# A planner's order with later loads, a table of 24 shifted tasks, and the last tile stored in two halves

## The chip, the cores and the metric

The kernel runs on one core of a Trainium2 chip. The metric is the time of one execution on the device in microseconds, the median of five runs. A profile is one further execution, taken by the hardware profiler; PE is the matrix engine (TensorE), DVE is VectorE, ACT is ScalarE, POOL is GpSimd, SP is SyncE, which issues most DMAs.

## What is computed

```python
for t in range(S):                                   # r, k, v: (4, 8, 768, 48); w, u: (8, 48)
    kt, vt, rt = k[:, :, t], v[:, :, t], r[:, :, t]
    cur = einsum('bhd,bhe->bhde', u * kt, vt)
    y[:, :, t] = einsum('bhd,bhde->bhe', rt, state + cur)
    state = w * state + einsum('bhd,bhe->bhde', kt, vt)
x = y.transpose(0, 2, 1, 3).reshape(4, 768, 384)
xn = (x - mean(x)) / sqrt(var(x) + 1e-6) * g_ln
out = x + maximum(xn @ w_ch1, 0) @ w_ch2             # w_ch1: 384 x 1536, w_ch2: 1536 x 384
```

A linear attention with a decaying state, then a layer norm and a two-layer network with a residual.

## The kernel before

The 4 x 768 rows are cut into 24 tiles of 128 tokens (i = 0 to 23, six to a batch). Within a tile the recurrence is written as matrix products: k and r are scaled by powers of the decay (tables Fk and Fr, made at the start from a scan, transposed on PE and copied to SBUF by ACT, L301 to L310), transposed, multiplied to a 128 x 128 score per head, masked, and multiplied with v; a 48 x 48 state per head goes from tile to tile.

For each tile the tasks are, in the names that the planner gives them: **k, r, v** loads (r for two tiles at once); **sck, scr** scale k and r (L365, L368); **TK, TR** transpose them on PE (L380, L394); **kT, rT** copy the transposed tiles out of PSUM (L386, L401); **vc** casts v to bf16 (L373); **q** multiplies r and k for the bonus term, **cc** sums it on PE, **cp** copies it out (L451), **Vb** multiplies v with it on POOL; **at** are the scores on PE (L417), **A** masks them on DVE; **kv** and **S, Z** update the state; **y** is the sum on PE (L508), **x** adds the bonus (L535). Then **xn** centres x, **sq** and **rs** give the variance, **ln** and **lc** transpose xn: for tiles under 8 on PE with a copy by ACT (L612), for the later ones as a DMA transpose that SP issues (L606). **up** g_m is one unit of the first product of group g (one tile for the first six groups, then two), six or twelve matmuls into a PSUM bank hp (L618); **re** is the relu that empties it, on ACT or DVE (L635); **dn** i m is a third of the second product of tile i, four matmuls of 384 columns (L649); **ot** scales and adds x on DVE (L662); **st** stores the tile (L673). The weights come in six loads, w1l and w2l, through four buffers, and are scaled or cast to bf16 in pieces (w1s, w2s). dn needs the matching third of w2.

PSUM has little room: one bank each for transposes (tr), scores (at), bonus and state (s), y and the second product (o), two for hp.

The order is not written by hand. Each task has an engine, a cost, needs, the buffers it takes and gives, a priority and sometimes other engines it may run on (alt). Planner.order (L47) is a list scheduler: again and again it takes the task that can start first by its costs, with the priority to break ties, puts it behind what its engine already has, and emits the instructions in that order. It runs when the kernel is built. On the chip every engine, SP's DMA queue too, works off its own list strictly in order, waiting on semaphores; so a task that waits for a load holds back everything after it on its engine. A load's end is planned as the time when the DMA engines have moved it plus `lands` (1.9 us, L109). SLK and SLT add a slack, which is 0 before. `after` holds a task back in the plan; it is no wait on the chip.

Where the plan leaves PE a gap before the first dn, matmuls on an identity are put in (keep_warm, L266 and L816 to L819).

Of the kernel before, what the change touches and what calls it, by code (L numbers as in the profile page):

```python
# [9 lines left out]
FP32 = mybir.dt.float32  # L10
# [4 lines left out]


RA = [("DVE", 0.64)]
SLK, SLT = 0.0, 35.0
PACE = 4.4


class Planner:
# [12 lines left out]
    def add(self, name, eng, cost, fn, needs=(), takes=(), gives=(), pri=0, load=0.0, kind=None,  # L35
            alt=None, lands=1.9, after=0.0):

        t = dict(name=name, eng=eng, cost=cost, fn=fn, needs=list(needs), takes=list(takes),  # L40
                 gives=list(gives), pri=pri, load=load, kind=kind, alt=alt, lands=lands, end=None,
                 first=(eng, cost), after=after)
        self.tasks.append(t)
        assert name not in self.by_name, name
        self.by_name[name] = t

    def order(self, patience=0.0, spread=0.0, seed=0):  # L47
# [14 lines left out]
        out = []  # L62
        while todo:
            best = None
            for t in todo:
                data = t["after"]
                ok = True
                for n in t["needs"]:
                    d = self.by_name[n]
                    if d["end"] is None:  # L70
                        ok = False
                        break
                    lag = 0.0 if d["eng"] == t["eng"] else self.LAG[d["eng"]]
                    if t["eng"] == "PE" and d["eng"] not in ("PE", "") and eng_at["PE"] > SLT:
                        lag += SLK
                    data = max(data, d["end"] + lag)
                if not ok:
                    continue
                for b, _, _ in t["takes"]:
                    if not free_at[b]:  # L80
                        ok = False
                        break
                    data = max(data, min(free_at[b]))
                if not ok:
                    continue
                pri = t["pri"] + vary[family[t["name"]]]
                if t["kind"] is not None and t["kind"] == last_kind:
                    pri -= 0.5
                pick = None
                for eng, cost in [(t["eng"], t["cost"])] + (t["alt"] or []):  # L90
                    ready = max(data, eng_at[eng] if eng else 0.0)
                    if t["load"]:
                        ready = max(ready, dma_at - (3.0 if eng == "SP" else 2.0))
                    if pick is None or ready + cost < pick[0]:
                        pick = (ready + cost, ready, eng, cost)
                key = (pick[1] - (patience * pri if pick[2] in ("DVE", "ACT", "POOL") else 0.0), -pri)
                if best is None or key < best[0]:
                    best = (key, t, pick)
            assert best is not None, [t["name"] for t in todo][:20]
            t, (_, t0, eng, cost) = best[1:]  # L100
            t["eng"], t["cost"] = eng, cost
            todo.remove(t)
            if t["kind"] is not None:
                last_kind = t["kind"]
            end = t0 + t["cost"]
            if t["eng"]:
                eng_at[t["eng"]] = end
            if t["load"]:
                dma_at = max(dma_at, end + 1.2) + t["load"]  # L109
                end = dma_at + t["lands"]  # L110
            t["start"], t["end"] = t0, end
            for b, owner, uses in t["takes"]:
                slots = free_at[b]
                slots.remove(min(slots))
                held[b, owner] = [uses, 0.0]
            for b, owner in t["gives"]:
                h = held[b, owner]
                h[0] -= 1
                h[1] = max(h[1], end)
                if h[0] == 0:  # L120
                    free_at[b].append(h[1] + self.LAG[t["eng"]])
            out.append(t)
# [4 lines left out]
def kernel(  # L127
# [173 lines left out]
    Fr = const.tile([P, 2, H, D], FP32, name="Fr")  # L301
    Fk = const.tile([P, H, D], FP32, name="Fk")
    LH = L // 2
    for j in range(3):
        fps = ps_h.tile([P, 512], FP32, name="hp") if j < 2 else ps.tile([P, 512], FP32, name="y")
        for kc in range(CK):
            src = T2[:, kc] if j == 2 else T[:, kc, j : 2 * L : 2]
            nc.tensor.transpose(out=fps[:, kc * P : (kc + 1) * P], in_=src, identity=ident_f[:])
        src = fps[:, :C].rearrange("p (h d) -> p h d", h=H)
        nc.scalar.copy(out=Fr[:, j] if j < 2 else Fk[:], in_=src)  # L310
    vec = const.tile([P, NR], FP32, name="vec")
    vps = ps.tile([P, 512], FP32, name="s")
    w_p, u_p = vec[:, CK : CK + HP], vec[:, CK + HP : NR]
# [80 lines left out]
    def transposes_r(e):  # L394
        sc = r_bufs[e % NSR].rearrange("p j (q e) d -> p j q (e d)", e=2)
        tp_t[e] = ps.tile([P, 2 * HP, P], BF16, name="tr")
        for j in range(2):
            for q in range(HP):
                nc.tensor.transpose(out=tp_t[e][:, j * HP + q, :], in_=sc[:, j, q, :], identity=ident[:])  # L399

    def evacuate_r(i, eng):  # L401
        e, c = divmod(i, 2)
        rT_t[i] = trp.tile([P, HP, P], BF16, name="rT", bufs=NRT)
        (eng.copy if eng is nc.scalar else eng.tensor_copy)(  # L404
            out=rT_t[i][:].rearrange("p q (t j) -> p q j t", j=2),
            in_=tp_t[e][:, :, c * LH : (c + 1) * LH].rearrange("p (j q) t -> p q j t", j=2),
        )
# [40 lines left out]
                skip_group_check=True,  # L448
            )

    def bonus_copy(i):  # L451
        cc_t[i] = sb2.tile([P, H], FP32, name="cc")
        nc.scalar.copy(out=cc_t[i][:], in_=s_t[i][:, C : C + H])  # L453

    def bonus_value(i):
        Vb_t[i] = sb2.tile([P, H, D], FP32, name="Vb")
# [152 lines left out]
            xT_t[g] = sb3.tile([P, CK, GW], BF16, name="xT")  # L609
        nc.sync.dma_start_transpose(out=xT_t[g][:, :, j * P : (j + 1) * P], in_=xn_t[i][:])  # L610

    def ln_evacuate(i):  # L612
        g, j = tile_group[i]
        nc.scalar.copy(out=xT_t[g][:, :, j * P : (j + 1) * P], in_=tp_t[i][:, :CK, :])

    hp_t = {}

    def up(g, m):  # L618
        gw = group_len[g] * P
        nf = 512 // gw  # L620
        if m == 0:
            hT_t[g] = sb3.tile([P, FK, GW], BF16, name="hT", bufs=NH)
        hp_t[g, m] = hp = ps_h.tile([P, 512], FP32, name="hp")
        for f in range(nf):
# [48 lines left out]
    def store(i, eng):  # L673
        b, c = divmod(i, NCH)
        eng.dma_start(out=out[b, c * L : (c + 1) * L, :], in_=ot_t[i][:])


    plan = Planner(
        dict(wst=NWS, sck=NSC, scr=NSR, r=LR, k=LD, vf=LD, vv=LD, tr=1, at=1, s=1, y=1, hp=2, o=1, kT=NKT, rT=NRT, q=2, A=2, cc=2, Vb=2,
             Z=3, S=2, x=NX, sum=4, sqs=4, sq=2, xn=3, xT=3, hT=NH, ot=3)  # L680
    )
    add = plan.add
    NU = {g: FK * n * P // 512 for g, n in enumerate(group_len)}
    add("scan", "DVE", 5.65, None, pri=99)
    add("Fr", "ACT", 5.9, None, pri=99)
    add("Fk", "ACT", 0.65, None, needs=["Fr"], pri=99)
    for name, lands in (("r0", 5.4), ("k0", 6.4), ("v0", 7.5), ("rows", 5.5)):
        add(name, "", lands, None, pri=99, takes={"r0": [("r", 0, 2)], "k0": [("k", 0, 1)], "v0": [("vf", 0, 2)]}.get(name, []))
    add("turn", "PE", 0.15, turn_rows, needs=["rows", "Fk", "TR0", "TK0"], pri=70, takes=[("s", "vec", 1)])
# [33 lines left out]
    for i in range(NT):  # L723
# [8 lines left out]
        if not half:  # L732
            add(f"scrb{e}", "", 0.0, None, [], [("scr", e, 1)], pri=p0)
            for t in range(2):
                add(f"scr{e}{t}", "POOL", 1.1, lambda g, e=e, t=t: scale_r(e, t, g), [f"r{e}", "Fr", f"scrb{e}"], [],
                    [("r", e)], pri=p0, alt=[("DVE", 0.7)])
            add(f"TR{e}", "PE", 0.46, lambda e=e: transposes_r(e), [f"scr{e}0", f"scr{e}1"], [("tr", ("r", e), 2)],
                [("scr", e)], pri=p0)
        add(f"rT{i}", "ACT", 0.74, lambda g, i=i: evacuate_r(i, g), [f"TR{e}"] + (["kT0"] if i == 1 else []), [("rT", i, 1)], [("tr", ("r", e))], pri=p0,
            alt=[("DVE", 0.74)])  # L740
# [3 lines left out]
                alt=[("DVE", 0.44)])  # L744
        else:
            add(f"kT{i}", "SP", 1.25, lambda i=i: transpose_k_by_dma(i), [f"sck{i}"], [("kT", i, 2)], [("sck", i)], pri=80,
                load=0.67, lands=3.0)
        add(f"vc{i}", "POOL", 0.6, lambda e, i=i: cast_v(i, e), [f"v{i}"] + ([f"kT{i}", f"rT{i}"] if i < 2 else []), [("vv", i, 1 if last else 2)],
            [("vf", i)], pri=p0, alt=[("ACT", 0.53), ("DVE", 0.42)])
        if qp(i):  # L750
# [2 lines left out]
        else:  # L753
# [2 lines left out]
        add(f"at{i}", "PE", 0.47, lambda i=i: scores(i), [f"kT{i}", f"rT{i}"], [("at", i, 1)], [("kT", i)], pri=p0 + 1)  # L756
        add(f"cc{i}", "PE", 0.13, lambda i=i: bonus(i), [f"q{i}", "uw"], [("s", i, 1 if last else 2)],
            [("q", i)], pri=p0 + 1)
        add(f"cp{i}", "ACT", 0.2, lambda i=i: bonus_copy(i), [f"cc{i}"], [("cc", i, 1)], [("s", i)], pri=p0 + 1)
        add(f"Vb{i}", "POOL", 0.85, lambda i=i: bonus_value(i), [f"cp{i}", f"v{i}"], [("Vb", i, 1)],  # L760
            [("cc", i), ("vf", i)], pri=p0 + 1)
        add(f"A{i}", "DVE", 1.22, lambda i=i: masked(i), [f"at{i}"], [("A", i, 1)], [("at", i)], pri=p0 + 1)
# [29 lines left out]
        if i < LNP:  # L792
            add(f"ln{i}", "PE", 0.18, lambda i=i: ln_transposes(i), [f"xn{i}", f"xT{g}"], [("tr", ("l", i), 1)],
                [("xn", i)], pri=p0 + 2)
            add(f"lc{i}", "ACT", 0.5, lambda i=i: ln_evacuate(i), [f"ln{i}"], [], [("tr", ("l", i))], pri=p0 + 2)
        else:
            add(f"lc{i}", "SP", 1.2, lambda i=i: ln_by_dma(i), [f"xn{i}", f"xT{g}"], [], [("xn", i)], pri=90, load=0.5, lands=3.0)
        for m in range(NM):
            add(f"dn{i}{m}", "PE", 0.66, lambda i=i, m=m: down(i, m),
                [f"re{g}_{u}" for u in range(NU[g])] + [f"w2s{m}{f}" for f in range(FS)] + ([f"dn{i}{m - 1}"] if m else []),  # L800
# [3 lines left out]
        add(f"st{i}", "SP", 0.55, lambda e, i=i: store(i, e), [f"ot{i}"], [], [("ot", i)], pri=99, load=0.6, lands=1.8,  # L804
            alt=[("ACT", 0.5)])
    for g, n in enumerate(group_len):
        for m in range(NU[g]):
            f0, f1 = m * FK // NU[g], (m + 1) * FK // NU[g] - 1
            w = sorted({f0 // FB, f1 // FB})
            add(f"up{g}_{m}", "PE", 0.66, lambda g=g, m=m: up(g, m),  # L810
                [f"lc{group_first[g] + j}" for j in range(n)] + [f"w1s{q}{kc}" for q in w for kc in range(CK)],
                [("hp", (g, m), 1)] + ([("hT", g, n)] if m == 0 else []), [("xT", g)], pri=-40, kind="u")
            add(f"re{g}_{m}", "ACT", 0.6, lambda e, g=g, m=m: relu(g, m, e), [f"up{g}_{m}"], [], [("hp", (g, m))], pri=30, alt=RA)
    pe_at = 6.1
    for t in plan.order():
        if t["eng"] == "PE":  # L816
            gap = t["start"] - pe_at - 0.1
# [36 lines left out]
```

## Time and profile before

| what | us |
|---|---|
| median of 5 runs (lowest to highest) | 158.59 (158.09 to 158.9) |
| the profiled execution | 159.96 |
| its span, first to last instruction | 158.2 |
| PE busy | 147.5 (93%), 1851 matmuls |
| of it warming matmuls | 12.8, 152 matmuls |
| DVE, ACT, POOL busy | 116.5, 97.3, 85.5 |
| granted clock of PE | 0.999 |

```profile
PE   5999999889999998989899959999999999999990
...
DMA  4999989999989989999798899212021211111122
```

The span is cut into 40 slices of about 4 us, and a digit is the busy share in tenths. PE is nearly full from the second slice on, with slices of 8 in between; the DMA engines are nearly full until slice 25, when the loads are done. Matmuls are pipelined and their ends are modelled, so the start to start distance of PE's rows is a better price than their duration. A row of the timeline is: start, duration, engine, line, operation, tiles, count, and in brackets the idle time before it and what ended it.

### The profile page before, as it was taken

Reading aid. Unit: us, or ns where it says so; the run is one execution under the profiler, and the core shown is the slowest. Engines: PE = TensorE matmul, PEld = TensorE weight load, DVE = VectorE, ACT = ScalarE, POOL = GpSimd, SP = SyncE. Lnnn points to the kernel's source line nnn. Section 1 sums busy time; section 2 is a strip of 40 time slices with the busy share of each in tenths; the row PEclk is TensorE's granted clock in tenths of the full one; section 3 lists DMA queues with packets and bytes.
Section 4 is the critical chain, followed back from the end, with each engine's and each line's share of the span. In section 5 each row is a group of like instructions: output and inputs, shape, how many; then the busy total and the mean of one; then the engine's idle time right before and its main releaser. Section 6 shows DMA issues by size and latency. Waiting matters only on the chain.

```text
span 158.2 us, 4634 instructions
## 1 busy us (share of the span) xinstructions
PE 147.5 (93%) x1851; PEld 115.8 (73%) x1851; DVE 116.5 (74%) x232; ACT 97.3 (62%) x217; POOL 85.5 (54%) x116
## 2 busy tenths in 40 slices
PE   5999999889999998989899959999999999999990
PEld 5899898668887776866677748787877777777650
DVE  5769999679798999888998949898999841001231
ACT  3558879757877686548877637677485454553100
POOL 7369598398647894695966668961642220000000
PEclk9999999999999999999999999999999999999999
DMA  4999989999989989999798899212021211111122
GB/s 98 233 227 341 348 164 265 377 188 182 250 195 240 229 192 176 235 234 212 154 240 173 186 204 206 77 29 75 4 85 64 57 47 49 50 54 50 50 99 99
DMA packets 75418, 25.46 MB, mean 161 GB/s; under 512 B 69632, under 2 KB 74246, under 8 KB 75398
## 3 DMA queue, kind: packets, MB, share of 16 engines
q1 hardware_dynamic: 72070, 23.21, 63.0%
q10 hardware_dynamic: 3232, 1.97, 4.1%
q8 instruction: 14, 0.23, 0.7%
q14 instruction: 6, 0.05, 0.1%
q0 software_dynamic: 96, 0.01, 0.1%
HBM read 18.88 MB, written 4.72 MB: 149 GB/s over the span
## 4 chain that ended last, share of the span: by engine, by line
PE 47%; DMA 27%; POOL 9%; SPq 8%; issue 3%; DVE 3%; ACT 1%; POOLq 0%; ACTq 0%
PE hp L627 18%; PE o L654 18%; DMA wst<-in_moe_w_ch_dram 11%; DMA v<-in_v_dram 11%; SPq L195 5%; DMA xT<-xn 3%; PE hp L654 2%; PE at L422 2%; DMA k<-in_k_dram 2%; POOL sc L369 2%; POOL Vb L457 2%; SPq L189 2%; PE y L525 1%; PE tr L399 1%; PE tr L384 1%
## 5 line engine op out<-in xcount | busy, mean ns | idle before, releaser
L627 PE MATMUL hp<-xT,w_sb 128*128 128x256 bf16 (+1 forms) x540 | 57.9, 251 | 0.7 <-DMA xT<-xn 0.6
L654 PE MATMUL o<-w_sb,hT 128*128 128x384 bf16 x264 | 52.1, 326 | 0.6 <-POOL w_sb L360 0.6
L627 PEld LDWEIGHTS <-w_sb 128*128 128x128 bf16 x540 | 43.4, 98 | 8.6 <-DMA xT<-xn 1.1
L641 ACT ACTIVATE hT<-hp 128x512 bf16<-128x512 f32 x60 | 35.5, 598 | 18.1 <-PE hp L627 17.5
L654 PEld LDWEIGHTS <-hT 128*128 128x128 bf16 x288 | 26.2, 98 | 13.6 <-issue 0.6
L664 DVE SCALAR_TENSOR_TENSOR ot<-o,rs,x 128x384 f32<-128x384 f32 x22 | 13.5, 612 | 22.4 <-PE o L654 22.3
L432 DVE TENSOR_TENSOR A<-at,mask 128x1024 bf16<-128x1024 f32 x24 | 29.2, 1215 | 0.5 <-PE at L422 0.4
L457 POOL TENSOR_TENSOR Vb<-v,cc 128x384 f32<-128x384 f32 x24 | 20.6, 856 | 9.1 <-ACT cc L453 9.1
L369 POOL TENSOR_TENSOR sc<-r,Fr 128x384 bf16<-128x384 f32 x18 | 19.8, 1112 | 7.9 <-ACT Fr L310 2.9
L366 POOL TENSOR_TENSOR sc<-k,Fk 128x384 bf16<-128x384 f32 x19 | 19.9, 1047 | 0.0
L565 ACT ACTIVATE sq<-x,sum 128x384 bf16<-128x384 f32 x24 | 14.6, 609 | 1.7 <-DVE x L538 1.6
L388 ACT COPY kT<-tr 128x512 bf16<-128x512 bf16 x22 | 12.9, 586 | 4.2 <-PE tr L384 3.1
L404 ACT COPY rT<-tr 128x512 bf16<-128x512 bf16 x17 | 11.8, 737 | 4.5 <-PE tr L399 2.8
L538 DVE SCALAR_TENSOR_TENSOR x<-y,Vb 128x384 f32<-128x384 f32 x24 | 13.1, 547 | 1.8 <-POOL Vb L457 1.4
L268 PE MATMUL o<-ident 128*128 128x128 bf16 x152 | 12.8, 240 | 1.6 <-DVE ident L243 1.6
L268 PEld LDWEIGHTS <-ident 128*128 128x128 bf16 x152 | 10.6, 109 | 1.9 <-DVE ident L243 1.6
L422 PE MATMUL at<-rT,kT 48*128 48x128 bf16 x192 | 9.5, 219 | 2.3 <-ACT kT L388 2.2
L422 PEld LDWEIGHTS <-kT 48*128 48x128 bf16 x192 | 5.4, 94 | 5.9 <-ACT kT L388 3.8
L643 DVE TENSOR_SCALAR hT<-hp 128x512 bf16<-128x512 f32 x12 | 8.2, 687 | 1.8 <-PE hp L627 1.7
L375 ACT CAST vv<-v 128x384 bf16<-128x384 f32 x10 | 5.1, 512 | 7.1 <-DMA v<-in_v_dram 7.0
L384 PE MATMUL tr<-ident,sc 128*128 128x128 bf16 x92 | 8.9, 219 | 0.5 <-DVE rT L404 0.5
L525 PE MATMUL y<-vv,A 128*128 128x48 bf16 x192 | 8.7, 183 | 0.4 <-DVE A L432 0.4
(87 smaller groups left out, 196.7 us busy)
## 6 DMA issues: line engine op xcount, KB each, us to landing
r<-in_r_dram SPq DMA_DIRECT2D x12, 384.0 KB, 5.0
k<-in_k_dram SPq DMA_DIRECT2D x24, 192.0 KB, 4.4
wst<-in_moe_w_ch_dram SPq DMA_DIRECT2D x6, 768.0 KB, 8.2
v<-in_v_dram SPq DMA_DIRECT2D x22, 192.0 KB, 4.1
out_dram<-ot SPq DMA_DIRECT2D x16, 192.0 KB, 3.0
out_dram<-ot ACTq DMA_DIRECT2D x8, 192.0 KB, 1.9
v<-in_v_dram ACTq DMA_DIRECT2D x2, 192.0 KB, 3.5
xT<-xn SPq DMA_TRANSPOSE x16, 3.0
```

The source lines that it names most:

```text
L268: nc.tensor.matmul(out=warm[:, :P], lhsT=ident[:], rhs=ident[:], start=True, stop=True)
L366: eng.tensor_tensor(out=k_bufs[i % NSC][:, :, :D], in0=k_t[i][:], in1=Fk[:], op=ALU.mult)
L369: eng.tensor_tensor(out=r_bufs[e % NSR][:, j, :, :D], in0=r_t[e][:, :, j * D : (j + 1) * D], in1=Fr[:, j], op=ALU.mult)
L422: nc.tensor.matmul(out=at_t[i][:, par, p, :], lhsT=kT_t[i][p0 : p0 + D, p, :], rhs=rT_t[i][p0 : p0 + D, p, :], start=True, stop=True,)
L432: nc.vector.tensor_tensor(out=A_t[i][:].rearrange("p e q t -> p (e q) t"), in0=at_t[i][:].rearrange("p e q t -> p (e q) t"), in1=mask[:].u ...
L457: nc.gpsimd.tensor_tensor(out=Vb_t[i][:], in0=vf_t[i][:], in1=cc_t[i][:].unsqueeze(2).to_broadcast([P, H, D]), op=ALU.mult)
L538: nc.vector.scalar_tensor_tensor(out=x_t[i][:], in0=y_t[i][:, :C], scalar=1.0, in1=Vb_t[i][:].rearrange("p h d -> p (h d)"), op0=ALU.mult, ...
L565: nc.scalar.activation(out=sq[:], in_=x_t[i][:], func=ACT.Square, bias=sum_t[i][:], scale=-float(C), accum_out=sq_t[e][:, c : c + 1],)
L627: nc.tensor.matmul(out=hp[:, f * gw : (f + 1) * gw], lhsT=w1_sb[:, n, kc, fb * P : (fb + 1) * P], rhs=xT_t[g][:, kc, :gw], start=(kc == 0) ...
L641: nc.scalar.activation(out=out, in_=src, func=ACT.Relu)
L654: nc.tensor.matmul(out=o_t[i][:, :C], lhsT=hT_t[g][:, fk, j * P : (j + 1) * P], rhs=w2_sb[:, fk, :], start=(fk == 0), stop=(fk == FK - 1),)
L664: nc.vector.scalar_tensor_tensor(out=ot_t[i][:], in0=o_t[i][:, :C], scalar=rs_t[i // 2][:, i % 2 : i % 2 + 1], in1=x_t[i][:], op0=ALU.mult ...
```

## The change

Five things change.
- The slack: SLK is 3.0 instead of 0, and is added where a planned task needs a load that was planned to start after 30 us (before: where PE needs another engine's result, after 35 us).
- A table SHIFT of 24 tasks: each has a shift of its priority, an earliest planned time, or one fixed engine.
- The start: the table copies become planned tasks that ACT or DVE can take; cp and lc can run on DVE too; a DMA transpose of k is planned to land later (no tile uses one).
- hT's buffer is taken when the first unit of a group is emitted, whichever unit it is, so the units of a group can change places; and TR of a pair waits in the plan for the TK before it, for tiles 9 and later.
- The last tile: its second product is made in two halves of 192 columns in hp banks, each finished and stored by itself.

```diff
-SLK, SLT = 0.0, 35.0
+SLK, SLT = 3.0, 30.0
+SHIFT = {
+    "up9_0": (0.0, 94.5, ""), "S15": (-4.2, 0.0, ""), "cp14": (0.0, 81.3, ""), "ln5": (0.0, 43.7, ""),
+    "re12_4": (0.0, 131.8, ""), "Vb2": (0.0, 25.0, ""), "dn52": (-5.3, 0.0, ""), "q19": (0.0, 103.6, ""),
+    "xn16": (0.0, 0.0, "DVE"), "x17": (0.0, 99.3, ""), "sq15": (0.0, 89.8, ""), "sck3": (0.0, 18.7, ""),
+    "dn32": (7.3, 0.0, ""), "y10": (0.0, 67.0, ""), "v13": (0.0, 52.8, ""), "TR2": (0.0, 27.7, ""),
+    "w1l0": (0.0, 11.3, ""), "v9": (0.0, 40.3, ""), "re7_1": (0.0, 73.1, ""), "Vb19": (0.0, 107.1, ""),
+    "rT5": (0.0, 0.0, "DVE"), "re13_1": (0.0, 0.0, "DVE"), "re9_1": (0.0, 0.0, "ACT"), "q21": (0.0, 114.6, ""),
+}
...
+        if name in SHIFT:
+            p, late, e = SHIFT[name]
+            t["pri"], t["after"] = pri + p, max(after, late)
+            for other in [t["first"]] + (alt or []):
+                if other[0] == e:
+                    t["first"], t["only"] = other, True
...
-                    if t["eng"] == "PE" and d["eng"] not in ("PE", "") and eng_at["PE"] > SLT:
+                    if d["load"] and d["lands"] == 1.9 and t["eng"] and d["start"] > SLT:
                         lag += SLK
...
-                for eng, cost in [(t["eng"], t["cost"])] + (t["alt"] or []):
+                for eng, cost in [(t["eng"], t["cost"])] + ([] if "only" in t else t["alt"] or []):
...
-        fps = ps_h.tile([P, 512], FP32, name="hp") if j < 2 else ps.tile([P, 512], FP32, name="y")
+        tab.append(ps_h.tile([P, 512], FP32, name="hp") if j < 2 else ps.tile([P, 512], FP32, name="y"))
...
-        nc.scalar.copy(out=Fr[:, j] if j < 2 else Fk[:], in_=src)
+
+    def copy_table(j, eng):
+        src = tab[j][:, :C].rearrange("p (h d) -> p h d", h=H)
+        (eng.copy if eng is nc.scalar else eng.tensor_copy)(out=Fr[:, j] if j < 2 else Fk[:], in_=src)
...
-        if m == 0:
+        if g not in hT_t:
             hT_t[g] = sb3.tile([P, FK, GW], BF16, name="hT", bufs=NH)
...
+    def down_half(h, m):
+        g, j = tile_group[NT - 1]
+        if m == 0:
+            oh_t[h] = ps_h.tile([P, 512], FP32, name="hp")
+        for fk in range(m * PM, (m + 1) * PM):
+            nc.tensor.matmul(
+                out=oh_t[h][:, :CH],
+                lhsT=hT_t[g][:, fk, j * P : (j + 1) * P],
+                rhs=w2_sb[:, fk, h * CH : (h + 1) * CH],
+                start=(fk == 0),
+                stop=(fk == FK - 1),
+            )
+
+    def finish_half(h):
+        i = NT - 1
+        oth_t[h] = sb2.tile([P, CH], FP32, name="oth")
+        nc.vector.scalar_tensor_tensor(
+            out=oth_t[h][:],
+            in0=oh_t[h][:, :CH],
+            scalar=rs_t[i // 2][:, i % 2 : i % 2 + 1],
+            in1=x_t[i][:, h * CH : (h + 1) * CH],
+            op0=ALU.mult,
+            op1=ALU.add,
+        )
+
+    def store_half(h, eng):
+        b, c = divmod(NT - 1, NCH)
+        eng.dma_start(out=out[b, c * L : (c + 1) * L, h * CH : (h + 1) * CH], in_=oth_t[h][:])
...
-    add("Fr", "ACT", 5.9, None, pri=99)
-    add("Fk", "ACT", 0.65, None, needs=["Fr"], pri=99)
+    add("first", "ACT", 4.95, None, pri=99)
+    add("rows0", "POOL", 4.9, None, pri=99)
+    for j, (name, done, bank_) in enumerate((("Fr0", 5.45, "hp"), ("Fr1", 5.85, "hp"), ("Fk", 6.2, "y"))):
+        add(f"t{name}", "", done, None, pri=99, takes=[(bank_, ("t", j), 1)])
+        add(name, "ACT", 0.5, lambda e, j=j: copy_table(j, e), [f"t{name}"], gives=[(bank_, ("t", j))], pri=99 - j, alt=[("DVE", 0.48)])
...
-            add(f"lc{i}", "ACT", 0.5, lambda i=i: ln_evacuate(i), [f"ln{i}"], [], [("tr", ("l", i))], pri=p0 + 2)
+            add(f"lc{i}", "ACT", 0.5, lambda e, i=i: ln_evacuate(i, e), [f"ln{i}"], [], [("tr", ("l", i))], pri=p0 + 2, alt=[("DVE", 0.36)])
...
-    pe_at = 6.1
+    pe_at = 6.3
```

In the built program the two orders differ on every engine from the first tiles on. Around the stalls that are spoken of below, PE's lists are (a digit pair after up and dn is group or tile and unit):

```
before: ln2 cc3 kv3 y3 TR2 up2_0 up2_1 TK4 up2_2 ln3 at4 dn00 cc4 kv4 TK5 up3_0 y4 at5 dn01 cc5 up3_1 dn02
after:  TK5 y3 ln2 TR2 dn00 up2_0 up2_1 at4 cc4 kv4 dn01 ln3 up2_2 y4 at5 cc5 dn02 up3_0 TR3 dn10 up3_1

before: TR7 up7_3 dn72 y13 up7_4 TK14 up7_5 up8_0 ... TK17 dn91 up9_0 y16 at17 dn92 cc17 TR9 up9_1
after:  TR7 dn72 y13 up7_4 TK14 up7_5 up8_0 ... TK17 dn92 up9_2 y16 at17 dn100 up9_3 dn101 up9_0 cc17 TR9 dn102 y17 up9_4 TK18

before, the end: dn202 dn212 dn230 dn220 dn221 dn222 dn231 dn232
after, the end:  dn202 dn212 dh00 dh01 dn220 dn221 dn222 dh02 dh10 dh11 dh12
```

ACT has sq15 vc21 cp16 kT17 re9_0 before, and cp16 kT17 vc21 re9_2 after; SP has v15 r8 lc9 k16 before and v15 r8 k16 lc9 after, and lc10 st6 k18 lc11 v18 before, k18 v18 st6 lc10 lc11 after. The warming matmuls are 152 before and 191 after.

## The prediction, made before the changed kernel had run

> **What bounds the kernel now.** I read the busy time by stage first, then PE's timeline, then the chain that ended last, then what each stall of PE waited for. By stage:
>
> ```profile
> core 0: us, PE busy (x) PEld busy (x) DVE busy (x) ACT busy (x) POOL busy (x), PEclk, DMA share, GB/s
> 8.00:31.00 23.00, 21.92 (x403) 19.86 (x401) 20.42 (x41) 18.41 (x41) 16.41 (x20) 1.00 1.02 286
> ...
> 80.00:94.00 14.00, 12.22 (x171) 9.37 (x170) 10.79 (x22) 9.10 (x22) 10.36 (x14) 1.00 0.93 193
> 94.00:154.40 60.40, 60.34 (x608) 45.20 (x606) 35.72 (x67) 31.20 (x66) 17.62 (x24) 1.00 0.24 70
> ```
>
> From 94 us to the end PE works 60.34 of 60.40 us: whatever PE has left at 94 us is paid in full. Until then the DMA share is near 1: the loads set the pace there, and PE idles. So the time is decided by how much PE work is done before the loads are in, and by the tail. The PE timeline names the idle time of the steady part:
>
> ```profile
> 61.80 0.40 PE L422 MATMUL at<-rT,kT 48*128 48x128 bf16 x8 [0.42 <-ACT kT L388]
> ...
> 69.37 1.48 PE L627 MATMUL hp<-xT,w_sb 128*128 128x256 bf16 x12 [0.49 <-DMA xT<-xn]
> ...
> 78.17 0.38 PE L384 MATMUL tr<-ident,sc 128*128 128x128 bf16 x4 [0.47 <-DVE rT L404]
> ...
> 79.37 0.83 PE L627 MATMUL hp<-xT,w_sb 128*128 128x256 bf16 x6 [0.15 <-DMA xT<-xn]
> ...
> 93.63 0.40 PE L422 MATMUL at<-rT,kT 48*128 48x128 bf16 x8 [1.78 <-ACT kT L388]
> ```
>
> Together 0.42 + 0.49 + 0.47 + 0.15 + 1.78 = 3.31 us. The last is the largest, and the chain shows that ACT was not slow; it stood in front of a load:
>
> ```profile
> 88.27 4.22 DMA v<-in_v_dram
> 92.53 0.12 issue
> 92.67 0.26 issue
> 92.93 0.16 ACT cc L453
> 93.09 0.50 ACT kT L388
> 93.63 0.40 PE at L422 x8
> ```
>
> ACT's cast of v (vc21) was queued ahead of the copies cp16 and kT17, which had nothing to do with it. The planner counted a load as landed 1.9 us after its data time; the issues part says 4.1 us from issue to landing for v. The other place is the early part:
>
> ```profile
> 29.89 0.40 PE L422 MATMUL at<-rT,kT 48*128 48x128 bf16 x8
> 30.89 0.82 PE L654 MATMUL o<-w_sb,hT 128*128 128x384 bf16 x4 [0.60 <-POOL w_sb L360]
> ```
>
> The first down-projection dn00 waits for w2, which lands at 30.1 us (POOL, DVE and ACT all sit idle for it until then); its casts are over at 31.0.
>
> **Part 1, the early order: a loss.** The built orders differ here. Before dn00 the old queue has TR0 to TR2, at0 to at4, y0 to y3 and all of up0, up1, up2; the new one puts dn00 ahead of up2_0, up2_1, at4, ln3 and up2_2 (Vb2 is held to 25.0 and TR2 to 27.7 in the table). From PE's timeline an up unit is 0.66, a down unit 0.65, at 0.33, y 0.37, TK 0.22, ln 0.17. So the new queue has 3 x 0.66 + 0.33 + 0.17 - 0.22 (TK5 comes earlier) = 2.26 us less done at dn00. Could dn00 start sooner instead? No: the loads up to w2 are the same, in the same order but for w1's two first parts, at a DMA share of 1.02, so w2 lands near 30.1 again. In the new queue w2's first four casts are two on ACT (0.93 from 30.1) and two on POOL (0.69 + 0.51), so dn00 can run at 30.9 to 31.3, and PE gets there at about 29.7 (11.5 us of work from TR0 at 8.4, 147 warming matmuls at 0.057 = 8.4, some 1.4 of waits for relu and xn). The hole shows as warming matmuls: 191 in the program, 152 before. Price at dn00: +2.3. Of it something returns: before, q5 on DVE stood behind a cast of w2 and cost PE 0.69 at 35.38; in the new order q5 is on POOL behind w2s20 (34.3 to 35.0, then 1.13 by the row of L415 on POOL, so 36.1), and PE reaches cc5 at 36.1 to 36.7: no wait, or a small one. I carry +1.7 to +1.8 from 44 us on (at6 at 44.1 with 1.49 us less work behind it; before 43.79). Bounds: +1.2 if half of the hole is filled, +2.7 if q5 is late.
>
> The table copies on DVE instead of ACT, and lc and cp with DVE as a choice, are a few instructions of 0.15 to 0.5 us; they lie before the wait for w2, so they are at nothing while it is there; without it they are worth at most the 0.4 us between Fr's two copies. Warming matmuls before TR0 (22, were 18) cost 0.2, under the same cover.
>
> **Part 2, slack behind loads: a gain.** I set each cast of v in both orders against the PE work queued before it. In the new order vc12 to vc23 stand 0 to 3.8 us of PE work later (vc16 +2.1, vc21 +2.8, vc23 +3.8), and PE itself is later in time by the 1.7 us. The longest wait for v before was 2.8 us. So:
> - at10 (0.42): vc13, which held DVE, is 2.6 us later: gone. Lag 1.7 - 0.42 = 1.3.
> - up7_0 (0.49): waits for the transpose lc9 on SP. SP is a queue too: k16 now stands ahead of lc9, and a k issue took 0.42 to 1.25, so it lands at 69.9 to 70.5, was 69.3. PE arrives at 68.9 + 1.3 = 70.2. I take 70.4: lag 1.0.
> - TK14 (0.47): the chain y12, x12 0.54, xn12 0.6, sq12 0.6, two rT copies 0.72 + 0.73, hops of 0.1 to 0.2, is about 3.9 us; PE has 1.75 to TR7's end and 1.68 after it (was 2.34, up7_3 has moved ahead). It still waits some 0.45: lag 1.0.
> - up8_0 (0.15): lc10 and lc11 now stand behind k18, v18 and st6. For lc11 only v18 is new: +0.5 to +1.0, landing 79.9 to 80.5. PE arrives at 80.2. I take 80.4: lag 1.05.
> - at17 (1.78): kT17 now stands ahead of vc21, and cp17 is on DVE. Behind vc21 is re9_2, and its waiter up9_0 comes 3.97 us of PE work after TK17: v21 may land as late as 95.2; expected 93.1 (92.5 and k22's 0.57 ahead of it). Gone: lag -0.73.
> - TK18, new: TR9 to TK18 has 1.68 us of work, was 3.7, for two rT copies in series (1.45) behind re9_0: +0.2. Lag -0.5.
> After that nothing in the order is tighter than what ran solid before. The table's other entries move a release time or an engine in the plan only, never a wait on the chip; what they do is in the order above, and past 94 us (re12_4, re13_1, dn52's and dn32's priorities, q19, q21) they shuffle work under a full PE: nothing, and at most one relu of 0.6 us if a bank of hp is then missing.
>
> **Part 3, the last tile.** The end:
>
> ```profile
> 153.08 1.31 PE hp L654 x8
> 154.42 0.62 DVE ot L664
> ```
>
> 24 matmuls of 192 columns replace 12 of 384. The page "TensorE: Matmul & The Clock Gate" of the Trainium skill ("Back-to-back issue gap") speaks against this: a stream of pairs of weight load and matmul is set by both, about 81 ns at 128 columns. By that, 192 columns cost at least 81 and I estimate 90 ns, so 24 x 90 - 12 x 163 = +0.2. The trace has 12 such pairs of 128 columns in 0.67 us, 56 ns each, so the weight load does not bind; by columns 24 x 82 = 1.97 against 1.95: nothing. I take the row. DVE: by the rows 128x384 (612 ns) and 128x1024 (1215) one column costs 0.94 ns, so half a tile saves 0.18. The store: "DMA: Bandwidth & Descriptors" ("Anatomy of one DMA", told there for GpSimd's path) holds about 2.0 us fixed whatever the size, so a half would save next to nothing; ACT's stores landed in 1.9 for 192 KB. At the page's best rate (377 GB/s in a slice) 96 KB are 0.25. Saving 0 to 0.3; I take 0.2. Half 0's store goes out on SP while half 1 still computes, so it is hidden. Sum -0.4.
>
> **Sum.** +1.7 - 0.42 - 0.3 + 0 + 0.05 - 1.78 + 0.2 - 0.4 = -0.95. The profiled execution took 159.96 for a span of 158.2; both lie around the median of the runs, 158.59, to which I apply the difference: 157.6.
>
> **Rivals.**
> A, PE never waits after 44 us: lc9 and lc11 land in time because PE is late, and TK14 and TK18 lose their waits: 1.7 - 3.31 - 0.4 = -2.0, so 156.6. For: PE is late by 1.7 at 44 us and the load stalls are fixed points in time. Against: the two rT copies in series.
> B, the hole is deeper: q5 on POOL, then Vb4 and scr31 behind it on the same queue, make cc5 and TR3 late; +2.7 instead of 1.7: 158.7, no change.
> C, slower: the xT transposes behind loads on SP. Transposes took up to 5.6 us to land, where lc9 took 4.36 and lc11 about 3.5. With 5.6 for both, lc9 lands at 71.6 (lag 2.2) and lc11 at 82.5 (lag 3.1); then -1.78 + 0.2 - 0.4 gives +1.1: 159.7. It decides from the point where lc11 lands after 81.3. For: SP is busy without a break from 69 to 78 us, DMA share 0.94. Against: the median landing is 3.0.
>
> **How the numbers follow.** The likeliest 0.42 (own range 156.9 to 158.3), A 0.20, B 0.15, C 0.23. The bound is 0.3%, 0.48 us, about what a measurement of this kernel tells from no change. Faster: 0.36 + 0.20 = 0.56; within: 0.06 + 0.10 = 0.16; slower: 0.05 + 0.23 = 0.28. The range goes from A less 0.6 to C plus 0.5: 156.0 to 160.2.
>
> **What would show it.** Right: dn00 at about 31 us with fewer up units ahead of it; at6 near 44; at17 without a wait for kT; no ACT wait for v over 1.5 us; last store landing about 1.7 us after issue. Wrong: w2 landing well before 30 (the hole is then small); up7_0 or up8_0 waiting over 1 us for xT; a new PE wait over 0.5 us after 94 us.

## The result and the profile after

| kernel | median us | lowest to highest | runs |
|---|---|---|---|
| before, beside it | 159.32 | 157.37 to 163.89 | 78 |
| after | 158.11 | 156.36 to 162.28 | 43 |

The ratio of after to before is 0.9925, with an interval of 0.9906 to 0.9944: 1.2 us less on the 158.59 us of the first five runs, so 157.4 against the forecast of 157.6. Measured twice more beside other kernels, the same change gave 0.9917 (0.9883 to 0.9951) and 0.9973 (0.9949 to 0.9997). Executions of one kernel lie 4 us and more apart, so the third decimal is not settled by one series. The forecast sum was -0.95 us, which is 0.9940.

The execution that was profiled for after was one of its slower ones, 160.01 us with a span of 158.0; a second profile of the same kernel (e2 below) took 156.52. Both are needed to read the change, and what only the recorded one shows is one draw out of five. First the busy time by stage of the recorded one, to be held against the rows that the prediction shows:

```profile
8.00:31.00 23.00, 22.78 (x413) 20.79 (x411) 18.79 (x43) 16.36 (x36) 16.73 (x21) 1.00 1.08 297
80.00:94.00 14.00, 12.17 (x157) 9.24 (x155) 10.58 (x20) 8.24 (x20) 8.59 (x14) 1.00 0.87 187
94.00:153.50 59.50, 59.50 (x624) 45.41 (x623) 37.24 (x75) 29.79 (x61) 18.48 (x25) 1.00 0.26 74
```

PE is busier up to 31 us (22.78 of 23.00, was 21.92), but with more warming matmuls in it. Past 94 us it is full, as before. In between, 80 to 94 us, it is no busier than before (12.17, was 12.22). PE's timeline says why: the waits have moved. (up7_0, TK14, up8_0 and up9_1 are the tasks of the four rows.)

```profile
69.60 1.48 PE L649 MATMUL hp<-xT,w_sb 128*128 128x256 bf16 x12 [0.49 <-DMA xT<-xn]
...
77.84 0.38 PE L405 MATMUL tr<-ident,sc 128*128 128x128 bf16 x4 [0.19 <-DVE rT L426]
...
79.65 0.82 PE L649 MATMUL hp<-xT,w_sb 128*128 128x256 bf16 x6 [0.77 <-DMA xT<-xn]
...
91.87 0.83 PE L649 MATMUL hp<-xT,w_sb 128*128 128x256 bf16 x6 [1.83 <-DMA xT<-xn]
```

The wait for kT at at17 (1.78 before) is gone, and in its place stand three waits for DMA transposes of xn, 3.09 us together. With the small ones the waits after 44 us sum to 3.58, against 3.31 before. In the second profile of the same kernel, the same stretch reads:

```profile
65.25 0.25 PE L464 MATMUL s<-uwI,q 128*128 128x2 bf16 x4 [0.30 <-DVE q L437]
...
76.95 0.38 PE L405 MATMUL tr<-ident,sc 128*128 128x128 bf16 x4 [0.19 <-DVE rT L426]
...
78.87 0.40 PE L444 MATMUL at<-rT,kT 48*128 48x128 bf16 x8 [0.23 <-ACT kT L409]
```

That is all: 0.72 us, and PE is busy for all of the stretch from 80 to 94 us:

```profile
80.00:94.00 14.00, 14.00 (x172) 10.93 (x170) 13.29 (x26) 9.27 (x22) 10.01 (x14) 1.00 0.89 190
```

So one kernel gives nearly the case of rival A in one execution and the mechanism of rival C in another, by when the transposes land. When they land goes with when SP comes to issue them. SP works its list in order; in the recorded profile it is 1.0 us behind e2 at 40 us and 3.7 us behind at lc13, the transpose that up9_1 waits for, while PE is 0.2 us behind at 42 us. First the recorded one, then e2:

```profile
87.12 1.35 SPq L632 DMA_TRANSPOSE xT<-xn  x1
```

```profile
83.42 1.40 SPq L632 DMA_TRANSPOSE xT<-xn  x1
```

Why SP fell behind in this execution is open.

The tail is the part that is the same in every execution. In the recorded one:

```profile
154.73 0.42 DVE L719 SCALAR_TENSOR_TENSOR oth<-hp,rs,x 128x192 f32<-128x192 f32 x1 [0.32 <-PE hp L708]
```

From PE's end to the span's end after has 3.26 us, before 3.79.

### The profile page after: what moved, and what is told of

Read it like the earlier page. It is cut to its first block, busy times and chain, and to the rows that moved or that the text cites. A ratio compares the mean times of both kernels' runs of the same rounds, so it can differ in the third digit from the quotient of the medians.

```text
span 158.0 us, 4730 instructions
## 1 busy us (share of the span) xinstructions
PE 148.8 (94%) x1902; PEld 118.6 (75%) x1902; DVE 120.1 (76%) x246; ACT 94.2 (60%) x205; POOL 84.8 (54%) x115
## 4 chain that ended last, share of the span: by engine, by line
PE 64%; SPq 13%; DMA 12%; DVE 6%; issue 2%; ACT 0%; DVEq 0%
PE o L676 23%; PE hp L649 23%; SPq L212 8%; DMA xT<-xn 7%; DMA wst<-in_moe_w_ch_dram 5%; SPq L206 3%; PE at L444 3%; PE y L547 2%; PE tr L420 2%; PE tr L405 2%; PE s L495 2%; PE y L535 2%; PE s L464 1%; PE hp L708 1%; PE hp L676 1%
## 5 line engine op out<-in xcount | busy, mean ns | idle before, releaser
L663 ACT ACTIVATE hT<-hp 128x512 bf16<-128x512 f32 x62 | 36.4, 594 | 26.3 <-PE hp L649 25.7
L676 PEld LDWEIGHTS <-hT 128*128 128x128 bf16 x276 | 25.4, 98 | 11.8
L454 DVE TENSOR_TENSOR A<-at,mask 128x1024 bf16<-128x1024 f32 x24 | 29.1, 1214 | 3.7 <-PE at L444 3.6
L390 POOL TENSOR_TENSOR sc<-r,Fr 128x384 bf16<-128x384 f32 x15 | 16.0, 1074 | 5.1 <-DVE Fr L330 3.0
L387 POOL TENSOR_TENSOR sc<-k,Fk 128x384 bf16<-128x384 f32 x16 | 17.2, 1078 | 0.0
L285 PE MATMUL o<-ident 128*128 128x128 bf16 x191 | 14.5, 231 | 1.6 <-DVE ident L260 1.6
L285 PEld LDWEIGHTS <-ident 128*128 128x128 bf16 x191 | 12.2, 104 | 1.9 <-DVE ident L260 1.6
L598 POOL TENSOR_SCALAR rs<-sqs 128x2 f32<-128x2 f32 x12 | 2.5, 210 | 17.1 <-ACT sq L587 16.8
L574 DVE TENSOR_SCALAR xn<-x,sum 128x384 bf16<-128x384 f32 x17 | 9.5, 560 | 0.1
L665 DVE TENSOR_SCALAR hT<-hp 128x512 bf16<-128x512 f32 x10 | 6.9, 689 | 3.0 <-PE hp L649 2.9
L601 POOL TENSOR_TENSOR rs<-rs,expo 128x2 f32<-128x2 f32 x12 | 8.6, 713 | 1.0
```

Of the source, the lines that this page charges most:

```text
L285: nc.tensor.matmul(out=warm[:, :P], lhsT=ident[:], rhs=ident[:], start=True, stop=True)
L387: eng.tensor_tensor(out=k_bufs[i % NSC][:, :, :D], in0=k_t[i][:], in1=Fk[:], op=ALU.mult)
L390: eng.tensor_tensor(out=r_bufs[e % NSR][:, j, :, :D], in0=r_t[e][:, :, j * D : (j + 1) * D], in1=Fr[:, j], op=ALU.mult)
L454: nc.vector.tensor_tensor(out=A_t[i][:].rearrange("p e q t -> p (e q) t"), in0=at_t[i][:].rearrange("p e q t -> p (e q) t"), in1=mask[:].u ...
L663: nc.scalar.activation(out=out, in_=src, func=ACT.Relu)
L676: nc.tensor.matmul(out=o_t[i][:, :C], lhsT=hT_t[g][:, fk, j * P : (j + 1) * P], rhs=w2_sb[:, fk, :], start=(fk == 0), stop=(fk == FK - 1),)
```

## The experiments

A ratio is to before on the same chip in the same series. There are three series: e1 to e4, e5 to e8 and e9 to e12, each on another chip; before had medians of 158.21, 157.55 and 157.66 us in them, so times and profiles of different series are compared with care. A planned order is a list of tasks, so an edit either changes the plan's input, and then everything may move, or moves tasks in the finished list, and then nothing else does. The two repeats come first.

**e1: before once more.**

> The kernel before once more, for a second profile. If the stall of 1.78 us at at17 and w2's landing at 30.1 us are properties of the order, both come again (1.3 to 2.0 us; 29.5 to 30.5). If they vary from run to run with the DMA engines, w2 lands up to 2 us elsewhere and the stall changes by over 0.7 us.

The profiled execution took 158.48 us, 1.5 less than the one that the prediction was made from. at6 is at 42.74, which was 43.79 there. The stall at at17 comes again:

```profile
92.16 0.40 PE L422 MATMUL at<-rT,kT 48*128 48x128 bf16 x8 [1.35 <-ACT kT L388]
```

The waits after 44 us sum to 3.01 (3.31 before), the tail is 3.78. The stall at at17 belongs to the order, then; the other waits differ from profile to profile (e4, which has the same order up to its last two tiles, has 2.63 in all). Of the 1.5 us, 1.05 lie ahead of at6, where loads land at other times.

**e2: after once more.**

> The changed kernel once more, timed and profiled. Both theories: 0.7 to 0.8% faster than before. Theory 'the xT wait of 1.83 us ahead of up9_1 is chance of that execution': it is under 0.8 us here and the span about 156. Rival 'it belongs to the order': 1.3 us or more again.

156.68 us, ratio 0.9917 (0.9883 to 0.9951). Its profile is shown above: the wait of 1.83 us at up9_1 did not come again. The early part of the timeline follows for after (recorded), for e2 and for e1. The first row of each is one of the first casts of w2, which say when w2 landed, and the last is dn00:

```profile
28.51 0.93 ACT L381 CAST w_sb<-wst 128x384 bf16<-128x384 f32 x2 [1.21 <-DMA wst<-in_moe_w_ch_dram]
...
29.30 0.81 PE L676 MATMUL o<-w_sb,hT 128*128 128x384 bf16 x4
```

```profile
27.25 1.07 POOL L381 CAST w_sb<-wst 128x384 bf16<-128x384 f32 x2
...
29.18 0.81 PE L676 MATMUL o<-w_sb,hT 128*128 128x384 bf16 x4
```

```profile
28.97 0.69 POOL L360 CAST w_sb<-wst 128x384 bf16<-128x384 f32 x1 [2.52 <-DMA wst<-in_moe_w_ch_dram]
...
30.19 0.82 PE L654 MATMUL o<-w_sb,hT 128*128 128x384 bf16 x4
```

w2 is there at 28.5 and 27.25 in the new order, at 30.1 (the prediction's profile) and 28.94 in the old one. Yet dn00 starts at 29.2 to 29.3 in both of the new ones, with no wait marked: e2's first casts are over at 28.3, and PE is at its warming matmuls and TR2 until 29.2. In e2 it is PE's own list that sets dn00. In the recorded profile dn00 starts 0.63 us after TR2, where e2 has 0.45, so there the casts may have held it by some 0.2 us; in the profile that the prediction read it was the load.

**e3: before, with vc21 alone moved behind kT17 in ACT's list.**

```diff
-    for t in plan.order():
+    todo = plan.order()
+    late = next(t for t in todo if t["name"] == "vc21")
+    todo.remove(late)
+    todo.insert(next(n for n, t in enumerate(todo) if t["name"] == "kT17") + 1, late)
+    for t in todo:
```

> The order before, with one ACT task moved: vc21, the cast of v for tile 21, goes behind kT17. Theory 'a load in front of kT17 costs the stall at at17': the 1.78 us shrink to under 0.4 and the time falls by 1.2 to 1.8 us. Rival 'the loads set the pace, the wait only moves on': the next consumer, re9_0 or TR9, waits instead and the time falls by less than 0.5 us.

157.92 us, ratio 0.9968 (0.994 to 0.9995): 0.5 us less, not the 1.2 to 1.8 that were expected. at17, at 90.00, no longer waits, but PE waits 3 us later for something else. DVE's two rows and PE's one:

```profile
92.24 0.56 DVE L538 SCALAR_TENSOR_TENSOR x<-y,Vb 128x384 f32<-128x384 f32 x1 [1.66 <-POOL Vb L457]
92.72 0.61 DVE L664 SCALAR_TENSOR_TENSOR ot<-o,rs,x 128x384 f32<-128x384 f32 x1
...
93.39 0.81 PE L654 MATMUL o<-w_sb,hT 128*128 128x384 bf16 x4 [1.03 <-DVE ot L664]
```

x16 waits on DVE for Vb16 from POOL, ot9 stands behind x16 on DVE, and the next down unit needs the bank that ot9 empties. And POOL seems to have been late for the same reason as ACT: it too had a cast of v in its list, which stood waiting for its load, and from there to Vb16 at 91.38 POOL is at work almost without a break:

```profile
86.46 0.50 POOL L375 CAST vv<-v 128x384 bf16<-128x384 f32 x1 [2.58 <-DMA v<-in_v_dram]
```

The stall at at17 had been cover for POOL. The cast in front of the copies was the cause of that wait, as the prediction said, but its whole length could not be had from that one move.

**e4: before, with the last tile by halves and nothing else.**

```diff
-    for t in plan.order():
+    todo = [t for t in plan.order() if t["name"] not in ("dn230", "dn231", "dn232", "ot23", "st23", "dn220", "dn221", "dn222", "ot22", "st22")]
...
+    todo += [dh[0, 0], dh[0, 1], by["dn220"], by["dn221"], by["dn222"], dh[0, 2], by["ot22"], by["st22"], oh[0], sh[0],
+             dh[1, 0], dh[1, 1], dh[1, 2], oh[1], sh[1]]
+    for t in todo:
```

dh are the thirds of a half's product on PE, oh its finish on DVE, sh its store, on SP for half 0 and on ACT for half 1.

> The order before up to the last two tiles, then the tail of the change: the last tile in two halves. Theory: 0.4 us faster (0.18 on DVE, 0 to 0.3 in the store, PE unchanged). Rival 'a DMA's cost is fixed and small matmuls are bound by weight loads': 0 to 0.2 us slower.

157.71 us, ratio 0.9944 (0.9914 to 0.9974): 0.9 us by the ratio, wider than what the trace holds. The tail went from 3.78 to 3.28, as in every kernel with halves (3.26 to 3.28 in eight of them, 3.31 in e7) against 3.78 or 3.79 in every kernel without. The at17 wait of before is there in full, as it must be:

```profile
91.85 0.40 PE L422 MATMUL at<-rT,kT 48*128 48x128 bf16 x8 [1.45 <-ACT kT L388]
```

**e5 and e10: after, with the last tile whole again** (the reverse of e4: dn230, dn220 to dn222, ot22, st22, dn231, dn232, ot23, st23). One kernel, in two series.

> The change without its tail: the changed order up to the last two tiles, then the last tile in one piece as before. Theory 'tail and order add up': 0.5 us slower than the changed kernel, so about 0.4% faster than before. Rival 'the tail is all of the gain': within 0.1% of before.

> The changed order with the last tile in one piece, now on the same chip as the changed kernel. Theory: the tail is worth what the traces show, 0.5 us, so this is 0.3% slower than the changed kernel and 0.4% faster than before. Rival 'the tail is all of the gain': 0.7% slower than the changed kernel, no different from before.

157.86 us, ratio 1.0023 (0.9998 to 1.0048), and 157.31 us, ratio 0.9992 (0.9966 to 1.0018). The new order by itself changes the time by nothing that these series tell from zero, as the rival had it ("the tail is all of the gain"), though both profiles show only 0.72 us of waits after 44 us. (PE ends at 151.0 and 151.5 in them, against e1's 152.9, but e1 is of the series in which before is slower by its median.) In the series of e10, after itself was 0.9973 (0.9949 to 0.9997).

**e6: after, with an empty table. e7: after, with SLK at 0.** Both are planned anew.

```diff
-SHIFT = {
...
-}
+SHIFT = {}
```

```diff
-SLK, SLT = 3.0, 30.0
+SLK, SLT = 0.0, 30.0
```

> The change with an empty table of shifts, planned anew. Theory 'the slack behind loads takes away the load stalls, the table only shuffles': within 0.3 us of the changed kernel, the early hole included (dn00 stays ahead of up2_0 in this order), no stall at at17. Rival 'the table does the work': back to before less the tail's 0.5 us, with PE waiting for copies behind loads again.

> The change with the slack at 0 but the table kept, planned anew. Theory 'the slack takes away the load stalls': stalls of 2 us or more between 44 and 95 us come back and it is 1 us or more slower than the changed kernel. Rival 'the slack is not needed once PE is late by a microsecond at 44 us': within 0.3 us of the changed kernel.

e6: 158.86 us, ratio 1.0088 (1.005 to 1.0125). e7: 159.54 us, ratio 1.013 (1.0083 to 1.0177). Each is slower than before, halves and all. The waits after 44 us are 1.46 in e6 and 2.54 in e7. They sit elsewhere than in either kernel; here first e6, then e7:

```profile
70.90 0.40 PE L437 MATMUL at<-rT,kT 48*128 48x128 bf16 x8 [0.68 <-ACT kT L402]
```

```profile
86.05 0.33 PE L535 MATMUL y<-Z,rT 128*128 128x96 bf16 x4 [0.46 <-DVE x L560]
...
87.19 0.37 PE L547 MATMUL y<-vv,A 128*128 128x48 bf16 x8 [0.81 <-DVE A L454]
```

So, with the other changes in place, the slack without the table is slower than before, and so is the table without the slack; both together lose nothing (e5, e10). The runs don't say which of the 24 entries matter, since each removal gives another plan. What e6 does say is that its order too has dn00 ahead of up2_0: the entries for Vb2 and TR2, which the prediction named, do not make the hole. Where e6's 0.9% comes from is not shown by its waits (1.46, less than before's 3.01 in e1); 0.2 us of it lie outside the span (see the end).

**e8: after, but with before's order of tasks up to dn42 (54 us).** EARLY is before's list of tasks, engines and planned times. It takes the hole away and leaves the later order.

```diff
...
-    pe_at = 6.3
-    for t in plan.order():
+    pe_at = 6.1
+    rest, todo = plan.order(), []
+    for name, eng, start, cost in [("Fr0", "ACT", 0.0, 0.5), ("Fr1", "ACT", 0.0, 0.5), ("Fk", "ACT", 0.0, 0.5)] + EARLY:
+        t = plan.by_name[name]
+        t["eng"], t["start"], t["cost"] = eng, start, cost
+        rest.remove(t)
+        todo.append(t)
+    for t in todo + rest:
```

> The order before up to dn42 (about 55 us), then the changed order with its tail: no early hole, late order as changed. Theory 'hole and later order are separate terms': up to 1.0 us faster than the changed kernel, the best of all. Rival 'the loads fix when the late stages run, so an early gain is given back by waiting': same as the changed kernel within 0.3 us, and the waits for v and xT in 60 to 95 us grow by what was gained.

156.87 us, ratio 0.9935 (0.9907 to 0.9962), within what after had in its three series (0.9917 to 0.9973). In its profile, what it gains early it loses at the transposes, as PE now gets there sooner. PE's two rows, then SP's two:

```profile
68.42 1.48 PE L734 MATMUL hp<-xT,w_sb 128*128 128x256 bf16 x12 [0.85 <-DMA xT<-xn]
...
78.87 0.82 PE L734 MATMUL hp<-xT,w_sb 128*128 128x256 bf16 x6 [1.16 <-DMA xT<-xn]
```

```profile
71.83 3.20 SPq L782 DMA_DIRECT2D out_dram<-ot  x1
75.12 2.50 SPq L717 DMA_TRANSPOSE xT<-xn  x2
```

SP's list is what holds them: one store took it 3.20 us to issue, and the transposes lc10 and lc11 left at 75.12, though xn10 and xn11 had been ready at 66.9 and 69.6. The waits after 44 us come to 3.27.

**e9: after a third time**, in one series with e10 to e12, so that they can be compared.

> The changed kernel a third time, beside its variants on one chip. 0.7 to 0.8% faster than before, as twice already. Rival: what differed between the two jobs so far is the chip, and it is within 0.4% here.

157.05 us, ratio 0.9973 (0.9949 to 0.9997), where 0.7 to 0.8% were expected: the rival came true, within 0.4% on this chip. After is here about as fast as in e2's series (medians 157.05 and 156.68); it is before that is 0.5 us faster. Its profile has 0.72 us of waits after 44 us, like e2's.

**e11: after, with the transposes ahead of the loads on SP. e12: e8 with the same.**

```diff
...
+    behind("lc9", "v15", "r8", "k16")
+    behind("lc11", "st5", "k18", "v18", "st6")
...
```

behind takes the named tasks out of the list and puts them right after its first name.

> The changed kernel with seven transfers moved on SP's queue: v15, r8 and k16 behind the transpose lc9; st5, k18, v18 and st6 behind lc10 and lc11. Theory 'the waits for xT come from loads ahead of them on SP': no wait for xT before up7_0 and up8_0, and 0.3 to 1.0 us faster in the median than the changed kernel. Rival 'the loads that were moved back are then late': waits for v or k of 0.5 us or more, same time or slower.

> The order before up to dn42, the changed order after it, and the transposes moved ahead as in the run before this one. Theory 'hole and xT waits are separate terms': 1.0 us faster than the changed kernel and the best of all. Rival 'an early gain is given back at the loads': no faster than the run before this one.

e11: 157.34 us, ratio 0.9976 (0.9946 to 1.0006), no different from e9. Its waits at up7_0 and up8_0 are gone (0.72 after 44 us), but that is what e9 has without the move. This profiled execution lost its time early, at TK4 and TK5, in a part that the edit does not touch:

```profile
25.63 0.40 PE L405 MATMUL tr<-ident,sc 128*128 128x128 bf16 x4 [0.77 <-POOL sc L387]
...
28.66 0.40 PE L405 MATMUL tr<-ident,sc 128*128 128x128 bf16 x4 [1.58 <-POOL sc L387]
```

e12: 156.35 us in six runs, ratio 0.9893 (0.9831 to 0.9955), the lowest of all, ahead of both kernels; its interval just overlaps that of e9 in the same series and overlaps e8's. The two waits of e8 are gone in its profile, and one is left. For up8_0 the move is seen to do it: lc10 and lc11 leave SP from 70.91 on, 4.2 us sooner than in e8. For up7_0 it is not, since PE came there at 69.00, 1.4 us later than in e8. That the move is worth time is not shown, as e8 and e12 are of different series.

```profile
89.56 0.83 PE L734 MATMUL hp<-xT,w_sb 128*128 128x256 bf16 x6 [0.69 <-DMA xT<-xn]
```

## Why the prediction was right, and where it was not

The time was right, and so was the direction, but that the sum came within 0.3 us is in part luck. Of the three parts only the tail came out as a sum that the trace repeats; in the other two the profiles have a smaller loss and, where the transposes land in time, about the gain that was forecast, and the timed runs don't show that gain. e2 is compared with e1 here, two executions of one series. They are not quite like: e1 lies 0.3 us above its kernel's median in that series and e2 0.2 below, so of the 1.96 us between them some 0.4 are the choice of the executions. PE's end is 152.92 in e1 and 151.20 in e2.

**Part 1, the hole.** Predicted +1.7, measured +1.0 (e2: at6 at 42.25 instead of 42.74, with 1.49 us less work behind it) and +1.2 (recorded profile, 42.47). Against the profile that the prediction read, which has at6 at 43.79, it is even -0.1 and +0.2. The 2.26 us less work at dn00 was right. The step that failed is "Could dn00 start sooner instead? No: ... w2 lands near 30.1 again". It landed at 27.25 and 28.5, and dn00 ran at 29.2, not 31. What was missed is that this landing is a draw. Over the twelve profiles of these two early orders the first cast of w2 is at 30.1, 28.9, 28.8, 29.1, 27.1 and 29.1 with the old early order (before, e1, e3, e4, e8, e12; 28.9 on average) and at 28.5, 27.3, 28.0, 28.0, 27.2 and 29.4 with the new one (after, e2, e5, e9, e10, e11; 28.1). The profile that the prediction read is the latest of the twelve, and e9, e10 and e11, with one early order on one chip, lie 2.2 us apart. What part of the 0.8 us between the averages is the order's is open, since the two sets overlap. It goes with when SP came to issue the first of w2's loads: at 21.6 to 21.9 us in the six profiles where w2 was there by 28.51, at 22.3 to 22.8 in the six where it was later, whichever the order. For e1 and e2 (w1's and w2's three loads are issued from one place each; these are w2's):

```profile
22.84 1.77 SPq L221 DMA_DIRECT2D wst<-in_moe_w_ch_dram  x3
```

```profile
21.89 1.93 SPq L238 DMA_DIRECT2D wst<-in_moe_w_ch_dram  x3
```

Five of the six early ones are of the new order and one of the old. That the order brings SP there sooner is likely, then, but not tried. The two executions that are compared here differ in how much the core moved shortly before, from 20 to 24 us; first e1, then e2:

```profile
20.00:24.00 4.00, 4.00 (x82) 3.79 (x80) 3.75 (x8) 3.30 (x8) 3.91 (x6) 1.00 0.75 152
```

```profile
20.00:24.00 4.00, 3.80 (x78) 3.40 (x76) 4.00 (x8) 3.40 (x7) 3.03 (x4) 1.00 1.02 197
```

The last two columns: a DMA share of 0.75 with 152 GB/s against 1.02 with 197. The prediction took the share of 1.02 of the whole stretch from 8 to 31 us for a sign that nothing could come sooner, and did not look at the dip within it (before has 0.83 there). So the prediction's own sign of error, w2 well before 30 and a smaller hole, is what came. That q5 on POOL would cost little was right: no wait at cc5 in either profile.

**Part 2, the stalls.** By rows:
- at10 (-0.42): right, no wait in the new order.
- up7_0 (0.2 left): none in e2 and e9, 0.49 in the recorded profile.
- TK14 (0.45 left): too high, 0.19 in all six profiles of the new order (after, e2, e5, e9, e10, e11).
- up8_0 (0.2 left): none in e2 and e9, 0.77 in the recorded profile. The forecast took one landing time for what differs from profile to profile.
- at17 (-1.78): right in every profile of the new order. e3 shows that the cast was the cause and that a single move gets 0.5 us of it, since POOL's Vb16 was as late. In the new order an ot stands ahead of x16 on DVE (e2: 90.82 and 91.91) and x16 has no wait, so the full amount went.
- TK18 (+0.2): no wait seen.
- Missed: cc11 0.30 and at14 0.23, which wait for DVE and ACT; and in the recorded profile up9_1, 1.83 for lc13, landed at 91.8.
The sum of waits in e2 is 0.72 against 3.01: -2.3, where the steps had -2.25. In the recorded profile it is 3.58, about what rival C has, but not as C has it: lc11 let up8_0 go at 79.65, before the 81.3 from which C was to decide, and the largest wait was lc13's, which C did not name.

**The table.** "They shuffle work under a full PE: nothing" holds for PE past 94 us, which is full. What the other entries do the prediction read off the built order. e6 adds that the table can't be left out: without it the planner builds another order, slower than before.

**Part 3, the tail.** Predicted -0.4, the trace has -0.51 in every profile with halves. DVE between PE's end and the store's issue: 0.69 to 0.49, -0.20 (forecast -0.18). The store's issue to its landing: 1.87 (155.07 to 156.94) in before, 1.62 (155.18 to 156.80) in after, -0.25 (forecast -0.2). The other 0.07 lie between that landing and the span's end. The prediction read the Trainium skill ("DMA: Bandwidth & Descriptors", "Anatomy of one DMA", told there for GpSimd's path) as leaving next to nothing for half a store, and this reading was wrong: the section adds to its fixed 2.0 us the bytes over 436 GB/s, by which I estimate 0.23 us for 96 KB less, and the trace agrees. What the trace does not have is the fixed 2.0 us for ACT's store: it is no more than some 1.4 us, if the 0.25 us for 96 KB are taken as proportional. (The 377 GB/s of the prediction is the best slice of before's profile.) PE's halves, the chain's last row in the recorded profile:

```profile
151.43 1.95 PE o L676 x12
153.38 1.33 PE hp L708 x16
```

16 halves take 1.33 us, 83 ns each, half of the 163 of a whole one: the row was right, and the pair of weight load and matmul, for which the Trainium skill has about 81 ns at 128 columns ("TensorE: Matmul & The Clock Gate", "Back-to-back issue gap"), did not add to it. In the timed runs the tail is worth 0.56% by e4, 0.2% by e9 against e10; the trace's 0.51 us is 0.32%.

**The sum again.** From e1 to e2: early +1.0, waits -2.3, tail -0.5, outside the span +0.3 (below), in all -1.5 where the two executions differ by 1.96; 0.4 us are spread over the rows and not attributed. By these steps the order without the tail should give -1.0 us, and e5 and e10 gave +0.2% and -0.1%. The spans of the timed runs say the same, as means over the executions that the ratios use: the order without the tail changes the span by +0.1 us in e5 and by -0.4 in e10, each uncertain by some 0.3, and adds 0.3 outside of it. The term outside the span was not in the prediction at all; it counted it as nothing by carrying the difference of spans over to the time. The recorded profile shows one way in which the rest of that gain can be lost, transposes that land late. It is one of five profiles of this order (after, e2, e5, e9, e10; the other four have 0.72 us of waits after 44 us), too few to say how often the timed runs see it, so this stays an argument. Most of the measured 1.2 us can be the tail's; the split between tail and order is not settled better than to some 0.5 us. That the early order by itself is a loss, as part 1 has it, is supported by e12, which has the old one: it took 0.7 us less than e9 by the medians, 1.3 by the ratios, with 0.2 of it outside the span, while moving the transposes alone did nothing that shows (e11). Six runs of e12 are too few to size it.

## What to carry to other kernels

When a list order is changed so that a copy no longer waits behind a load, look at what the old stall covered on the other engines: taking one cast out of the way bought 0.5 us of a 1.35 to 1.78 us stall, because another engine stood behind a load as well. A time at which a load landed in one profile is a draw; before a step is built on it, see by how much it differs between profiles of the same kernel, here 1.2 us between two, and look at when the queue came to issue it. Transposes that PE needs soon can be put ahead of loads that nobody needs yet on a queue; here that took a wait away where PE got there early (up8_0, from e8 to e12) and changed nothing where it did not (e9 to e11), and no time was shown to be saved by it.

## What was not expected of the hardware

The time outside the span is not the same for the two kernels. An execution of before is longer than its span by 1.78 to 1.79 us, and so are e4, e8 and e12 (1.79) and e3 (1.81). With the early orders that the new code plans it is 1.94 to 2.06 (after, e2, e6, e7, e9, e10, e11) and 2.78 in e5. The timed runs repeat it: the mean is 1.79 in before and 2.0 in after, with at most 1.87 in any of before's 151 runs in the three series. In the trace's DMA records after and e2 have a fetch of 8 KB of instructions that begins 1.8 us after the last instruction of the program (e2: 156.25 to 156.76, the span ends at 154.47); before has none there, and its last transfer is the store. The same fetch is in all eight profiles with the longer time, and in none of the six with 1.78 to 1.81. e5 has besides it one of 16 KB, from 156.52 to 157.81. So an order can cost 0.2 to 1 us outside its span, which no sum over the span's rows contains; that the fetch is the cause is likely from this, not tried. The program with more warming matmuls is the longer one (1902 matmuls against 1851), but what decides whether such a fetch comes late was not tried.

One store took SP 3.20 us to issue in e8, and single transposes 1.2 to 3.3 us (e3 has the longest): SP's list is a queue of its own that what stands behind has to wait for.
